# Products of zeros in TensorE's waits, 256-wide chunks in both halves, and a new written order for an attention and two-MoE kernel

## The chip, the core and the metric

The kernel runs on one core of one Trainium2 chip. Its time is device microseconds, from three runs of the kernel before, and one further execution was profiled. A core has TensorE (PE; its weight loads are shown apart as PEld), VectorE (DVE), ScalarE (ACT), GpSimd (POOL) and SyncE (SP), which here issues every DMA. A matrix product writes to PSUM, the accumulators beside it.

## What is computed

Three parts follow each other, all in float32. The inputs q, k, v are 2 batches x 8 heads x 576 positions x 64.

```python
q_d = q.reshape(B, H, Sd, factor, D).mean(axis=3)      # factor = 4; k_d, v_d likewise
out_up = np.repeat(sm_attn(q_d, k_d, v_d), factor, axis=2)
mask = np.abs(pos[:, None] - pos[None, :]) < factor     # a band of 7 positions
out_local = softmax(where(mask, scale * q @ k.T, -1e9)) @ v
x = (out_up + out_local), as 1152 tokens x 512
...
h = x @ w_in                                            # 512 x 2048
x = (h * sigmoid(h)) @ w_out                            # 2048 x 512
...
for e in range(4):                                      # second mixture, w1 512 x 1024, w2 1024 x 512
    out += p[:, e:e+1] * (relu(x @ w1[e]) @ w2[e])
```

## The kernel before

**Products in three passes.** An operand of a large product is split into a high part (fp32r) and the rest: `x` is `xh` and `xl`, a weight is `wh` and `wl`. One product is then three on TensorE: high by high, high by low, low by high (`mm3`, line 603, and line 690 in `quarter`).

**Attention** is cut into 16 jobs, numbered 0 to 15: two batches, two stretches of queries (c = 0 with 256 queries, c = 1 with 320), four pairs of heads. Each job is a round through all engines, whose steps have one letter each, with the job's number behind it:

- S: scores of the band on TensorE and the mask added there (lines 403, 410). x: row maximum and subtraction on DVE (418, 419). e: exp on ACT (424). u: sum on DVE (427).
- q, k, p: q and k summed by fours, q on DVE for the first four jobs, the rest on POOL (365, 342). v: the same for v on POOL. D: scores of the pooled q and k on TensorE (444, 448). n: their maximum on DVE (463, 464). d: their exp on ACT (465).
- r: reciprocals and normalising on DVE (471 to 478). g: the same for the pooled ones on ACT (480). T: transposes on TensorE (490, 492). a: copies of these out of PSUM on ACT (493 to 500).
- V: the values, on TensorE (518, 522). o: a copy on ACT (525). f: the two attentions added on DVE (527). h and l: the sum split into `xh` on ACT and `xl` on DVE (534, 535). tD, tT and the like are the pooled rest of a batch.

**Weights** of the first mixture come as 8 units of 4 pieces, each piece 128 x 512 words of 64 bits, whose two halves hold one float32 weight in a wider form. A piece n (n = 4 x unit + place) is loaded into a stage buffer (`in_s`n) of which there are three, and unpacked in `split_raw`: A on ACT (236), the low word by Z on ACT (242) or, for n in `LOW_ON_DVE`, by B on DVE (239), C on DVE (244), which joins both in a `dec` tile, w on ACT (250) for the high part, L on POOL (251) for the low part.

**The first mixture** runs in two halves of the 2048 columns, each in four chunks of tokens. M and G are products of the first matrix, H of the second: G`c`_`ft`_`k` is chunk c (0 to 3 in half 0, 4 to 7 in half 1), block ft of 128 columns, quarter k of the depth. th, gf, gh and gl are the steps behind a G block (tanh, the product, the split), ya, yf, yh and yl those behind an H block. In half 0 the chunks are 256, 320, 256 and 320 tokens wide, in half 1 256, 256, 256 and 384. M0 to M3 are the blocks of chunk 0 that need one head pair each. Chunks 0 and 1 are done in `quarter` in two parts, so that they can begin while attention still runs.

**The order of the work** around the change is written out by hand. `WRITTEN` holds one list of step names for each of SP, TensorE, ACT, DVE and POOL; `written(names)` chains each step to the one before it, and every engine runs its steps strictly in that order. The lists reach to chunk 5. What is after them (the rest of half 1 and the four experts of the second mixture, lines 603, 843 to 892) is ordered by priorities.

PSUM is shared out as three `mm` tiles, two `s` tiles (scores), `t1` and `t2` (transposes) and `o` (values), each of 128 x 512 float32. A step that writes a tile waits until the tile's last user is done.

Of the kernel before, what the change touches and what calls it, by code (L numbers as in the profile page):

```python
# [62 lines left out]
def attention_moe_kernel(ctx, tc, kqa, kqb, qtl, va, vb, w64, w1d, w2d, dpr, out):  # L63
# [596 lines left out]
    def quarter(ci, p, o, n):  # L660
        c = slice(o, o + n)
        g = [4 * ci + i for i in range(4)]
        two = n == 256
# [15 lines left out]
        for sums in groups:  # L679
            first = {}  # L680
            for i in range(4):
                wh, wl = parts(2 + p, i)
                for d, ps in sums:
                    if not two or len(sums) == 4:
                        next_step(0.125)
                    s = slice(d * 128, d * 128 + 128)
                    h, l = gh[g[i]][:, 0:n], gl[g[i]][:, 0:n]
                    for x, (a, y) in enumerate(((wh, h), (wh, l), (wl, h))):
                        z = two and d % 2
                        m = PE.matmul(out=ps[:, 0:n], lhsT=a[:, s], rhs=y, start=(not z and i == 0 and x == 0),  # L690
                                      stop=(i == 3 and x == 2), skip_group_check=True)
                        if i == 0 and x == 0:
                            first[d] = m
                            if z:
                                after(m, first[d - 1])
                        mark(f"H{ci}_{d}_{4 * p + i}", m)
                if i:
                    attn_tick()
            for d, ps in sums:
                ya = acc[:, d * NT + o:d * NT + o + n]  # L700
                if p == 0:
                    i = ACT.activation(out=ya, in_=ps[:, 0:n], func=ACTF.Copy, scale=0.5)
                else:
                    i = DVE.scalar_tensor_tensor(out=ya, in0=ps[:, 0:n], scalar=0.5, in1=ya, op0=ALU.mult, op1=ALU.add)
                mark(f"ya{ci}_{d}_{p}", i)
# [496 lines left out]
```

## Time and profile before

| what | us |
|---|---|
| median of three runs | 646.92 |
| lowest and highest of them | 645.60 and 648.19 |
| the profiled execution, device time | 649.48 |
| its span, first to last instruction | 647.7 |
| TensorE busy | 629.0 (97%) |
| DVE, ACT, POOL busy | 415.4, 325.3, 249.1 |

The profile is one execution. The page slices the span into 40 equal parts of 16.2 us and gives each a digit, the busy share in tenths. The chain of waits is followed back from the last instruction, at each step to what released it. A timeline row has its start and length in us, the engine, the line, the operation and its tiles, how many such instructions it merges, and in brackets how long the engine was idle before it and what ended that. TensorE's ends are modelled, so the rate of dense products is read from the chain, as the time of many over their number.

### The profile page before, as it was taken

What the parts mean: (1) busy time and instruction counts of PE and PEld (TensorE: products, weight loads), DVE (VectorE), ACT (ScalarE), POOL (GpSimd) and SP (SyncE); (2) the same over time, 40 slices, a digit from 0 to 9 for tenths busy, and PEclk for the clock granted to TensorE, in tenths of its full rate; (3) what the DMA queues carried; (4) which work ended last, traced back from release to release, by engine and by line L of the source; (5) the groups of instructions that cost most, each with busy time, mean ns of one, the idle gap of its engine ahead of it and who ended that gap; (6) DMA issues with size and microseconds to landing.
All of it is one profiled execution on the core that took longest, in us unless ns stands there. A gap on an engine that the chain in (4) does not pass through costs nothing.

```text
span 647.7 us, 13723 instructions
## 1 busy us (share of the span) xinstructions
PE 629.0 (97%) x5492; PEld 617.6 (95%) x5492; DVE 415.4 (64%) x859; ACT 325.3 (50%) x746; POOL 249.1 (38%) x353
## 2 busy tenths in 40 slices
PE   4989999999999999999999999999999999999995
PEld 3779999999999999999999999999999999999995
DVE  5878676547445737756668954769855579755534
ACT  2788776578725525443346533355533366433321
POOL 7567532034400004443646412654433564333210
PEclk9789999999999999999999999999999999999998
DMA  8955551235600400420013300024200020001001
GB/s 276 285 164 187 175 173 56 78 100 163 194 2 1 132 1 1 162 67 2 1 34 108 113 9 1 1 67 131 66 1 2 1 66 1 1 33 35 2 32 50
DMA packets 16928, 48.17 MB, mean 74 GB/s; under 512 B 2976, under 2 KB 4256, under 8 KB 16864
## 3 DMA queue, kind: packets, MB, share of 16 engines
q1 hardware_dynamic: 16864, 47.29, 23.4%
q8 instruction: 43, 0.70, 0.5%
q14 instruction: 21, 0.17, 0.1%
HBM read 44.93 MB, written 2.36 MB: 73 GB/s over the span
## 4 chain that ended last, share of the span: by engine, by line
PE 94%; DVE 3%; ACT 2%; DMA 1%; issue 0%; POOL 0%; ACTq 0%
PE mm L603 57%; PE p L864 27%; PE mm L690 4%; PE s L403 2%; PE o L522 1%; PE t L490 1%; PE o L518 1%; DVE acc L892 1%; DMA kq<-in_kqa_dram 1%; PE mm L993 1%; PE s L410 1%; PE s L448 0%; PE t L492 0%; ACT dec L236 0%; PE mm L403 0%
## 5 line engine op out<-in xcount | busy, mean ns | idle before, releaser
L603 PE MATMUL mm<-xh,wbuf 128*128 128x256 f32 (+2 forms) x1248 | 259.6, 292 | 0.0
L603 PEld LDWEIGHTS mm<-xh,wbuf 128*128 128x128 f32 x1248 | 203.7, 188 | 0.1
L603 PE MATMUL mm<-xl,wbuf 128*128 128x256 f32 (+2 forms) x624 | 182.0, 292 | 0.0
L849 POOL TENSOR_TENSOR r<-r 128x128 f32<-128x128 f32 x160 | 95.0, 606 | 177.4 <-ACT r L843 133.1
L852 DVE TENSOR_TENSOR h<-r,h 128x384 fp32r<-128x384 f32 (+1 forms) x128 | 91.6, 718 | 65.7 <-ACT h L851 65.4
L851 ACT ACTIVATE h<-r 128x384 fp32r<-128x384 f32 (+1 forms) x128 | 73.3, 578 | 93.5 <-POOL r L849 54.5
L603 PEld LDWEIGHTS mm<-xl,wbuf 128*128 128x128 f32 x624 | 117.1, 188 | 0.0
L864 PE MATMUL p<-wext,h 128*128 128x256 f32 x672 | 89.2, 276 | 0.0
L864 PE MATMUL p<-wbuf,h 128*128 128x256 f32 x672 | 82.7, 276 | 0.0
L864 PEld LDWEIGHTS p<-wext,h 128*128 128x128 f32 x672 | 82.2, 188 | 0.0
L864 PEld LDWEIGHTS p<-wbuf,h 128*128 128x128 f32 x672 | 79.4, 188 | 0.0
L603 PE MATMUL mm<-gh,wbuf 128*128 128x256 f32 (+2 forms) x384 | 77.1, 292 | 0.0
L603 PEld LDWEIGHTS mm<-gh,wbuf 128*128 128x128 f32 x384 | 62.0, 188 | 0.0
L843 ACT ACTIVATE r<-mm 128x512 f32<-128x512 f32 x48 | 28.6, 596 | 65.4 <-PE mm L603 64.7
L849 DVE TENSOR_TENSOR r<-r 128x128 f32<-128x128 f32 x96 | 39.3, 410 | 34.0 <-ACT r L843 29.4
L603 PE MATMUL mm<-gl,wbuf 128*128 128x256 f32 (+2 forms) x192 | 55.8, 291 | 0.0
L631 DVE TENSOR_TENSOR gl<-gf,gh 128x256 fp32r<-128x256 f32 (+2 forms) x64 | 34.2, 540 | 18.1 <-ACT gh L630 17.7
L625 DVE SCALAR_TENSOR_TENSOR gf<-th,mm 128x256 f32<-128x256 f32 (+2 forms) x64 | 28.7, 451 | 23.6 <-ACT th L624 21.6
L251 POOL TENSOR_TENSOR wbuf<-dec,wbuf 128x512 fp32r<-128x512 f32 x24 | 31.0, 1301 | 26.4 <-ACT wbuf L250 20.4
L892 DVE SCALAR_TENSOR_TENSOR acc<-p,pr,acc 128x256 f32<-128x256 f32 (+1 forms) x63 | 36.1, 605 | 3.6 <-PE p L864 3.0
L794 POOL TENSOR_TENSOR wext<-kst,wext 128x512 fp32r<-128x512 f32 x8 | 10.4, 1300 | 69.5 <-ACT wext L792 46.9
L630 ACT ACTIVATE gh<-gf 128x256 fp32r<-128x256 f32 (+2 forms) x64 | 28.0, 442 | 16.5 <-DVE gf L625 15.7
(173 smaller groups left out, 1035.2 us busy)
## 6 DMA issues: line engine op xcount, KB each, us to landing
stg<-in_w_dram SPq DMA_DIRECT2D x29, 512.0 KB
kst<-in_w2d_dram SPq DMA_DIRECT2D x16, 512.0 KB
kst<-in_w1d_dram SPq DMA_DIRECT2D x12, 512.0 KB
kq<-in_kqb_dram SPq DMA_DIRECT2D x8, 323.0 KB
kq<-in_kqa_dram SPq DMA_DIRECT2D x6, 419.0 KB
stg<-in_w1d_dram SPq DMA_DIRECT2D x4, 512.0 KB
acc<-in_w_dram SPq DMA_DIRECT2D x3, 512.0 KB
vw<-in_vb_dram SPq DMA_DIRECT2D x8, 180.0 KB
```

What stands on the lines that cost most here:

```text
L251: mark(f"L{4 * u + j}", POOL.tensor_tensor(out=l, in0=d, in1=h.bitcast(F32), op=ALU.subtract))
L603: ins = [PE.matmul(out=ps, lhsT=l, rhs=r, start=(first and i == 0), stop=(last and i == n - 1)) for i, (l, r) in enumerate(pairs)]
L625: mark(f"gf{c}_{ft}", DVE.scalar_tensor_tensor(out=gf[:, 0:n], in0=th[:, 0:n], scalar=1.0, in1=ps[:, 0:n], op0=ALU.add, op1=ALU.mult))
L630: latest[ACT] = mark(f"gh{c}_{ft}", ACT.activation(out=gh[g][:, 0:n], in_=gf[:, 0:n], func=ACTF.Copy))
L631: latest[DVE] = mark(f"gl{c}_{ft}", DVE.tensor_tensor(out=gl[g][:, 0:n], in0=gf[:, 0:n], in1=gh[g][:, 0:n].bitcast(F32), op=ALU.subtract))
L690: m = PE.matmul(out=ps[:, 0:n], lhsT=a[:, s], rhs=y, start=(not z and i == 0 and x == 0), stop=(i == 3 and x == 2), skip_group_check=True)
L843: ACT.activation(out=r[:, 0:4].rearrange("p s t -> p (s t)"), in_=ps[:, 0:512], func=ACTF.Relu)
L849: latest[eng] = eng.tensor_tensor(out=r[:, o], in0=r[:, a], in1=r[:, b], op=op)
L851: ACT.activation(out=h, in_=r[:, part], func=ACTF.Copy)
L852: latest[DVE] = DVE.tensor_tensor(out=l, in0=r[:, part], in1=h.bitcast(F32), op=ALU.subtract)
L864: ins = [PE.matmul(out=ps, lhsT=x, rhs=y, start=(opens and k == 0 and i == 0), stop=(k == 3 and i == n - 1), skip_group_check=True) for i, ...
L892: DVE.scalar_tensor_tensor(out=o, in0=ps, scalar=p, in1=o, op0=ALU.mult, op1=ALU.add)
```

## The change

Four things change.

1. **Chunks.** Both halves now use 256, 256, 256 and 384 tokens. `quarter` loses its form for 320 tokens, with its groups of three and one PSUM tiles; four 256-wide sums now share two tiles in both of its chunks. The tiles `gh`, `gl`, th and gf are opened 256 wide, and 384 wide from the last chunk of half 0 on.
2. **Products of zeros.** `fill(name, t)` issues `FILL[name]` matrix products of a 128 x 128 by a 128 x 256 bf16 tile of zeros ahead of a step, into the PSUM tile that the step is about to write. There are 39. The zeros lie in an unused part of `acc`, cleared on DVE by the first step there, `cw`.
3. **Unpacking.** Pieces 16 to 31 (units 4 to 7) take their low word by B on DVE instead of Z on ACT. For these units the `dec` tile is gone: A writes to the upper words of the stage buffer, and C, w and L work on it there.
4. **Written order.** All five lists are new, and reach one chunk further, to the new chunk 5 and the loads and splits of the first expert weights (`in_w9_1`, `in_k0_0` to `in_k0_2`, `hw`, `lw`).

```diff
-XN = (256, 320, 256, 320)
-
-CHUNKS = (tuple(zip(XOFF, XN)), ((0, 256), (256, 256), (512, 256), (768, 384)))
+CHUNKS = ((0, 256), (256, 256), (512, 256), (768, 384))
...
-LOW_ON_DVE = (0, 1, 2, 3)
+FILL = {"S2": 4, "S4": 4, "V0": 6, "T1": 5, "V2": 2, "S6": 1, "T5": 3, "V5": 5, "T6": 9}
+LOW_ON_DVE = (0, 1, 2, 3) + tuple(range(16, 32))
...
-            d = d_p.tile([128, 512], F32, tag="dec", name="dec")
+            d = d_p.tile([128, 512], F32, tag="dec", name="dec") if u < 4 else v[:, :, 1].bitcast(F32)
...
+    zeros = acc[:, 4470:4598].bitcast(BF16)
+
+    def fill(name, t):
+        for _ in range(FILL.get(name, 0)):
+            mark(name, PE.matmul(out=t, lhsT=zeros[:, 0:128], rhs=zeros, start=True, stop=True, skip_group_check=True))
+
     def constants():
+        mark("cw", DVE.memset(zeros, 0.0))
...
+        fill(f"S{j.i}", j.ps[:, 0:256])
...
+        fill(f"T{j.i}", t1[:, 0:2].rearrange("p a b -> p (a b)"))
...
+        fill(f"V{j.i}", o[:, 0:256])
...
-        two = n == 256
...
-        if two:
-            b = [mm_tile() for _ in range(2)]
-            groups = [[(d, half(b[d // 2], d % 2)) for d in range(4)]]
-        else:
-            groups = [[(d, mm_tile()) for d in ds] for ds in ((0, 1, 2), (3,))]
+        b = [mm_tile() for _ in range(2)]
+        sums = [half(b[d // 2], d % 2) for d in range(4)]
...
-    open_g(320)
+    open_g(256)
...
+            if hf == 0 and lastc:
+                m1ctx.close()
+                open_g(384)
...
-            if (hf, ci) == (1, 1):
+            if (hf, ci) == (1, 2):
                 for names in WRITTEN:
                     written(names)
...
-        if hf == 0:
-            m1ctx.close()
-            open_g(384)
```

The beginnings of the five lists, SP, TensorE, ACT, DVE and POOL in turn:

```diff
-        """in_kq0 in_kq1 in_s0 in_kq2 in_vg0 in_kq3 in_vg1 in_kq4 in_kq5 in_vw0 in_s1 in_qt in_vg3 in_vw1 in_s3 in_vg2 in_vw2
-        in_s2 in_kq6 in_s8 in_s10 in_vw3 in_kq7 in_s9 in_vg8 in_vw4 in_kq12 in_vw5 in_kq8 in_s11 in_vg9 in_kq9 in_s4
+        """in_kq0 in_kq1 in_s0 in_s1 in_kq2 in_kq3 in_kq4 in_vg0 in_vg1 in_vw0 in_s2 in_kq5 in_vw1 in_vw2 in_s3 in_qt in_s9
+        in_vg2 in_vg3 in_s8 in_vw4 in_kq6 in_vw5 in_s10 in_vw3 in_kq7 in_vg8 in_kq8 in_kq12 in_s11 in_kq9 in_vw6 in_vg9
...
-        """S0 S1 D0 D1 S2 S3 T0 D2 S4 V0 S5 T1 D3 D5 D4 V1 M0 T2 M1 V2 T3 tD S6 T4 V3 D6 S7 M2 tT M3 V4 T5 D7 S8 T6 V5 D8
-        H0_0_0 H0_2_0 H0_3_0 S9 H0_1_0 H0_0_1 H0_2_1 V6 T7 G1_0_0 H0_1_1 D9 H0_3_1 G1_0_1 G1_0_2 V7 S10 H0_0_2 H0_2_2 T8
+        """S0 S1 D0 S2 D1 S3 T0 S4 D2 V0 T1 S5 D4 V1 D3 M0 T2 D5 M1 V2 T3 tD S6 T4 M2 V3 S7 D6 tT T5 V4 D7 M3 S8 V5 S9 T6 D8
+        H0_0_0 H0_1_0 H0_2_0 H0_3_0 T7 V6 H0_0_1 G1_0_0 G1_0_1 H0_2_1 H0_1_1 H0_0_2 H0_1_2 G1_0_2 H0_3_1 V7 S10 D9 T8
...
-        """e0 A0 e1 d0 d1 e2 g0 a0 tab w0 o0 d2 g1 e3 A1 h0 e4 e5 a1 w1 d3 o1 d4 g2 h1 a2 d5 g3 A2 g4 A3 o2 a3 Z8 w3 h2 g5
+        """tab A0 e0 A1 e1 w0 d0 g0 d1 g1 e2 a0 w1 d2 e3 o0 e4 h0 A2 a1 A3 o1 e5 h1 d3 g2 d4 w2 a2 d5 Z9 g3 g4 o2 A8 a3 h2 g5
...
-        """x0 q0 q1 x1 n0 cz B0 C0 n1 q2 u0 r0 x2 u1 q3 r1 x3 n2 x4 f0 u2 B1 x5 C1 l0 n3 r2 n4 u3 f1 n5 u4 l1 r3 r4 u5 B3 r5
+        """cw cz q0 q1 x0 B0 x1 C0 B1 n0 C1 q2 u0 r0 n1 x2 u1 r1 x3 n2 x4 B2 f0 u2 q3 r2 l0 x5 n4 B3 f1 n3 C2 u3 l1 u4 n5 r3
...
-        """cb ci cq cm k0 k1 v0 k2 v1 k3 p4 p5 tp L0 L1 v2 v3 L3 p6 L2 p7 L8 v8 p8 L9 p9 L10 v9 L11 p10 p11 L4 v10 v11 L6 L5
+        """cq cb cm ci k0 k1 L0 k2 v0 p4 v1 L1 k3 p5 tp v2 L2 v3 L3 p6 p7 L9 v8 p8 L8 v9 L10 p9 v10 L11 p10 p11 L5 L4 p12 L6
```

## Rows read from the trace of the kernel before

**Rows 1.** The page's slices of the span: TensorE busy, its granted clock, transfers.

```profile
PE   4989999999999999999999999999999999999995
...
PEclk9789999999999999999999999999999999999998
...
GB/s 276 285 164 187 175 173 56 78 100 163 194 2 1 132 1 1 162 67 2 1 34 108 113 9 1 1 67 131 66 1 2 1 66 1 1 33 35 2 32 50
```

**Rows 2.** Busy us by stage: PE, PEld, DVE, ACT, POOL, granted clock, DMA share, GB/s.

```profile
4.00:16.00 12.00, 7.88 (x80) 5.58 (x80) 8.44 (x21) 3.50 (x9) 9.26 (x16) 1.00 1.00 318
16.00:24.00 8.00, 7.33 (x82) 5.73 (x82) 5.76 (x17) 4.55 (x14) 2.78 (x8) 0.57 0.96 264
24.00:37.00 13.00, 10.65 (x155) 9.09 (x152) 11.57 (x39) 11.86 (x35) 10.17 (x13) 1.00 0.60 203
...
48.00:123.00 75.00, 75.00 (x830) 70.70 (x831) 53.66 (x140) 55.28 (x153) 31.91 (x47) 1.00 0.45 140
...
123.00:180.00 57.00, 56.96 (x458) 56.53 (x457) 29.48 (x55) 42.99 (x94) 20.63 (x16) 1.00 0.45 140
```

**Rows 3.** The chain of waits, TensorE's dense stretches: start, us, what.

```profile
108.57 5.29 PE mm L690 x36
...
302.90 2.72 PE mm L603 x24
...
350.74 4.16 PE mm L603 x24
```

**Rows 4.** Timeline of ACT, the first exp.

```profile
6.97 1.28 ACT L424 ACT_TABLE_LOAD   x1 [6.97 <-DVE s L419]
8.27 0.39 ACT L424 ACTIVATE s<-s 128x280 f32<-128x280 f32 x1
```

**Rows 5.** Timeline of DVE, unpacking: lines 239 (B) and 244 (C).

```profile
10.04 1.24 DVE L239 TENSOR_SCALAR stg<-stg 128x512 int32<-128x512 int32 x1
...
11.39 1.56 DVE L244 SCALAR_TENSOR_TENSOR dec<-dec,stg 128x512 int32<-128x512 int32 x1
...
22.04 0.42 DVE L239 TENSOR_SCALAR stg<-stg 128x512 int32<-128x512 int32 x1
...
23.84 0.68 DVE L244 SCALAR_TENSOR_TENSOR dec<-dec,stg 128x512 int32<-128x512 int32 x1
```

**Rows 6.** Timeline of TensorE: S0, T0, V0, M0, S6, the first H.

```profile
4.37 1.20 PE L403 MATMUL s<-kq 64*64 64x70 f32 x16 [4.37 <-DMA kq<-in_kqa_dram]
...
15.02 0.63 PE L490 MATMUL t<-ident,sm 128*70 128x128 f32 x4 [1.88 <-DVE sm L478]
...
19.49 0.70 PE L518 MATMUL o<-atd,vd 72*64 72x64 f32 x8
...
26.15 0.39 PE L993 MATMUL mm<-xh,wbuf 128*128 128x256 f32 x1
...
31.90 0.83 PE L403 MATMUL s<-kq 64*64 64x70 f32 x20
...
48.25 0.38 PE L690 MATMUL mm<-gh,wbuf 128*128 128x256 f32 x1
```

**Rows 7.** The chain of waits, M2 and M3.

```profile
38.79 2.15 PE mm L993 x12
41.16 1.38 PE mm L993 x12
```

**Rows 8.** Timeline of POOL: a v step, an L step, the last eight L.

```profile
9.96 1.04 POOL L342 TENSOR_TENSOR vg_f<-vg_f 72x512 f32<-72x512 f32 x1 [1.52 <-DMA vg_f<-in_va_dram]
...
33.53 1.28 POOL L251 TENSOR_TENSOR wbuf<-dec,wbuf 128x512 fp32r<-128x512 f32 x1 [2.29 <-ACT wbuf L250]
...
158.59 2.56 POOL L251 TENSOR_TENSOR wbuf<-dec,wbuf 128x512 fp32r<-128x512 f32 x2 [3.10 <-ACT wbuf L250]
...
172.44 2.54 POOL L251 TENSOR_TENSOR wbuf<-dec,wbuf 128x512 fp32r<-128x512 f32 x2 [1.58 <-ACT wbuf L250]
```

**Rows 9.** Groups by line: Z.

```profile
L242 ACT ACTIVATE stg<-stg 128x512 int32<-128x512 uint16 x26 | 17.4, 674 | 2.2 <-DMA stg<-in_w_dram 2.2
```

More of the change, by code (lines that the diff above doesn't have):

```diff
@@ L257, in split_raw @@
             c = slice(j * 1024, (j + 1) * 1024)
-            behind(ACT, ACT.activation(out=h[:, c], in_=t, func=ACTF.Copy))
-            behind(DVE, DVE.tensor_tensor(out=l[:, c], in0=t, in1=h[:, c].bitcast(F32), op=ALU.subtract))
+            mark(f"hw{u}_{j}", ACT.activation(out=h[:, c], in_=t, func=ACTF.Copy))
+            mark(f"lw{u}_{j}", DVE.tensor_tensor(out=l[:, c], in0=t, in1=h[:, c].bitcast(F32), op=ALU.subtract))
     actx = ExitStack()
@@ L672, in quarter @@
         flush()
-        if two:
-            b = [mm_tile() for _ in range(2)]
-            groups = [[(d, half(b[d // 2], d % 2)) for d in range(4)]]
-        else:
-            groups = [[(d, mm_tile()) for d in ds] for ds in ((0, 1, 2), (3,))]
-        step[0] -= 0.5
[L679 to L705, printed above, removed]
@@ new lines, in quarter @@
+        b = [mm_tile() for _ in range(2)]
+        sums = [half(b[d // 2], d % 2) for d in range(4)]
+        step[0] -= 0.5
+        first = {}
+        for i in range(4):
+            wh, wl = parts(2 + p, i)
+            for d, ps in enumerate(sums):
+                next_step(0.125)
+                s = slice(d * 128, d * 128 + 128)
+                h, l = gh[g[i]], gl[g[i]]
+                for x, (a, y) in enumerate(((wh, h), (wh, l), (wl, h))):
+                    m = PE.matmul(out=ps, lhsT=a[:, s], rhs=y, start=(d % 2 == 0 and i == 0 and x == 0),
+                                  stop=(i == 3 and x == 2), skip_group_check=True)
+                    if i == 0 and x == 0:
+                        first[d] = m
+                        if d % 2:
+                            after(m, first[d - 1])
+                    mark(f"H{ci}_{d}_{4 * p + i}", m)
+            if i:
+                attn_tick()
@@ L707, in g2_evac @@
+        for d, ps in enumerate(sums):
+            ya = acc[:, d * NT + o:d * NT + o + n]
+            if p == 0:
+                i = ACT.activation(out=ya, in_=ps, func=ACTF.Copy, scale=0.5)
+            else:
+                i = DVE.scalar_tensor_tensor(out=ya, in0=ps, scalar=0.5, in1=ya, op0=ALU.mult, op1=ALU.add)
+            mark(f"ya{ci}_{d}_{p}", i)
     def g2_evac(hf, db, c, ps, n):
@@ L775, in split_u @@
             with at_prio(tick_of(e, 0, k) - LEAD_USPLIT):
-                ACT.activation(out=h[:, c], in_=t[:, c], func=ACTF.Copy)
+                mark(f"uh{e}_{k}_{c.start}", ACT.activation(out=h[:, c], in_=t[:, c], func=ACTF.Copy))
                 eng = POOL if k in U_LO_POOL else DVE
-                eng.tensor_tensor(out=l[:, c], in0=t[:, c], in1=h[:, c].bitcast(F32), op=ALU.subtract)
+                mark(f"ul{e}_{k}_{c.start}", eng.tensor_tensor(out=l[:, c], in0=t[:, c], in1=h[:, c].bitcast(F32),
+                                                               op=ALU.subtract))
         held[i] -= 1
@@ new lines, in attention_moe_kernel @@
+        C6 gl1_2 x12 gf1_3 n11 f9 C7 u11 gl1_3 r11 l9 gf0_4 n12 C13 u12 C12 gl0_4 f10 gf0_5 r12 l10 x13 gf0_6 gl0_5 gf0_7
+        nt1 gl0_7 C14 rt1 C15 gf1_4 gl0_6 x14 gf1_5 ya0_2_1 f11 ya0_3_1 gl1_4 l11 n13 gl1_5 gf1_6 n14 ya0_0_1 B16 gl1_6
+        gf1_7 u13 gl1_7 ya0_1_1 r13 ya1_0_1 ya1_1_1 f12 B17 x15 gf2_0 l12 u14 n15 gf2_1 r14 gl2_0 gl2_1 u15 f13 gf2_2 C16
+        r15 gf2_3 B18 gl2_2 l13 gf2_4 ya1_2_1 ya1_3_1 gl2_3 f14 gf2_5 C17 gl2_5 l14 C18 gl2_4 gf2_6 gf2_7 f15 gl2_6 gl2_7
+        l15 B20 B19 C19 C20 B21 gf3_0 C21 gf3_1 gl3_0 gl3_1 gf3_2 gf3_3 gl3_3 gf3_4 gl3_4 B22 C22 gf3_5 gl3_2 gf3_6 B23
@@ L989, in start_mm @@
             hold.extend(mm_tile() for _ in range(2))
+            fill("M0", hold[0][:, 0:256])
         for i in range(4):
@@ L1053, in attention_moe_kernel @@
                         load_piece()
-        for ci, (o, n) in enumerate(CHUNKS[hf]):
+        for ci, (o, n) in enumerate(CHUNKS):
             if hf == 0 and ci < 2:
                 continue
-            lastc = ci == len(CHUNKS[hf]) - 1
+            lastc = ci == len(CHUNKS) - 1
+            if hf == 0 and lastc:
+                m1ctx.close()
+                open_g(384)
             main_at[1] = 4 * hf + ci
```

100 lines of the change are left out of this document (52 added, 48 removed).

## The prediction

> **What bounds the kernel now.** I read the page's slices first, then the stages, then the chain of waits and the timelines of the first 50 us. The reader is to see that TensorE is full in every slice but the first, the third and the last, that its granted clock is below full only near the start (0.7 and 0.8 in the second and third slice), and that the transfers run at 276 GB/s there [rows 1]. The stages say where time can still be won [rows 2]: from 48 us on TensorE is busy to within 0.04 us, so the end moves only with the work that it is given there; before 48 us it idles, or runs slowly, for part of the time. In 24:37 ACT (11.86 of 13.00) and DVE (11.57) are nearly full, but in 16:24 they are not (4.55 and 5.76 of 8.00), and in 4:16 ACT is busy for 3.50 of 12.00. The ramp up to the first H product at 48.25 [rows 6] is therefore bound first by a chain of steps through all engines, and then by ACT and DVE.
>
> The profiled execution took 649.48 us, 647.7 of them span. The median of the runs shown is 646.92. I work the sum in microseconds off the profiled execution and take it off the median unscaled.
>
> **Chunk widths.** The 384 products of half 0 that are 320 wide become 192 of 256 and 192 of 384; half 1 is unchanged, and so is the number of products. The chain of waits, where it is dense, gives 5.29/36 = 147 ns for 320, 2.72/24 = 113 ns for 256 and 4.16/24 = 173 ns for 384 [rows 3]. Before: 384 x 147 = 56.4 us. After: 192 x (113 + 173) = 55.0. This stands on the dense path: **-1.4 us**.
>
> **Table load.** ACT loads its table only when the first exp is due: 6.97 to 8.25, and the exp starts at 8.27; what released the load was DVE's subtraction for that same exp [rows 4]. With `tab` first in ACT's order, after the DVE memset `cz`, the load falls into the empty microseconds before the first scores at 4.37 [rows 6]: -1.3 on the first chain. It is the first term of the ramp, not to be added to it. The one load of the trace is followed at once by the exp, so nothing but its 1.28 us is on the path. The Trainium skill, ScalarE: Activation LUTs, "What ACT_TABLE_LOAD costs", adds a drain of 1.38 us to a load of 1.28; the row agrees with the load and shows no drain on the path. By that page the gain would be 2.7 and the forecast 1.4 lower, 640.1; I take the row.
>
> **The order of the ramp**, walked step by step through the new orders with the old durations.
> - First scores: S0 and x0 stay, e0 comes at about 7.4 behind A0 instead of 8.27, D0 at 7.85. DVE now has B0, x1, C0 and B1 ahead of n0; at 0.42 for a B and 0.68 for a C [rows 5] n0 starts near 9.2 and the first normalised scores are ready at 11.8. Before, T0 waited for them until 15.02 [rows 6], as B0 and C0 took 1.24 and 1.56 there while POOL added v [rows 5, 8].
> - T0 stands behind S2, D1 and S3. s1, now fourth on SP instead of eleventh, delays kq2 by its 128 x 512 words of 8 bytes, 0.52 MB, at 276 GB/s [rows 1]: 1.9 us. So S2 starts at 9.6, S3 ends near 13, T0 starts at 13.1: 1.9 us ahead of 15.02 [rows 6].
> - V0: S4 and its four zero products follow T0 instead of D2; v0 waits for vg0, which lands some 4.6 us later (s1, kq3 and kq4, 1.28 MB, pass it), and ends at 15.1. V0 starts at 16, 3.5 ahead of 19.49 [rows 6].
> - M0: l0 has fewer steps ahead of it on DVE (C1 and the maximum after S5 have moved) and ends by 19.5. M0 then waits for D3, whose k3 is queued behind L0 and L1 on POOL at 1.28 each [rows 8]: 21.1 against 26.15 [rows 6].
> - From there the shift can't grow, for ACT and DVE are full. A3 waits some 0.3 us on ACT for s3; v2 waits on POOL for vg2, with L2 and v3 queued behind it. On SP kq8 is moved ahead of kq12, which waits there for kq6's buffer and held up all loads behind it, so S8 no longer waits for that. M3 comes at 36.5 (before 41.16 [rows 7], less what runs ahead of it), the first H product at 42.7 against 48.25.
> So the walk gives 5.6 us at that product, and S9 (at most 0.83, what 20 products took at full clock [rows 6]) has by then been done too: 6.4. Against it I set 1.7 us, since two DVE steps were that much longer beside POOL [rows 5] and four such steps now stand there, and 0.7 us for late landings and steps that just miss. **-4.0 us**. The bounds are -1.3 (the table load alone, then ACT and DVE full as before) and -6.4.
>
> **Zero products.** 39 products of 256 columns, written to a tile that the next step overwrites. I price one by the 113 ns row, 4.4 us in all, or at the lower clock by M2's twelve in 2.15 [rows 7], 0.18 each, 7.0 us. They wait for the PSUM tile and not for the data, so they lie in front of steps whose data come later: S2 for kq2, V0 for a0 and v0, T6 for D8's p8 behind it. What covers them is the lateness of DVE, ACT and POOL; where that is gone they cost their full price and S4, T1 or V5 is late next. What they may give is the clock: in 16:24 it was 0.57 of full [rows 2], that is 6.9 of the 8 us at 1.2 GHz and the rest at 2.4, after 12 us in which TensorE had been busy for 7.88; and M2 took 2.15 against M3's 1.38 [rows 7]. My walk has full clock from about 12.5, so both the price and the gain are in it. Bounds of this item: 7.0 lost; gained 3.4 (half of the 6.9) and 0.8 (M2).
>
> **Edits at nothing.** B16 to B31 put 16 x 0.42 = 6.7 us on DVE and take 16 x 0.67 [rows 9] off ACT. All of it is in 123:180, where DVE has 29.48 of 57.00 and TensorE is full [rows 2]. A writes in place at a stride; Z does that already [rows 9], so no price. But a stage buffer is now held until L on POOL (1.28) instead of until C. The last eight L took from 158.59 to 174.98 [rows 8], 2.05 each; w and L, 1.9 us more for one of three buffers, make it 2.7, 21.6 for the eight of units 6 and 7. Between the G3 products that free their place and chunk 4's H products, their users, stand H3's 96 products at 173 ns and G4's at 113, 27.5 us. Bounds 0 and 2 us late; I take 0, for the rest that this leaves. The wider g pool is opened one chunk earlier; it makes the first gh of chunk 3 wait for the last H of chunk 2 in place of the same wait one chunk later, and the new order has G3 products between them. The longer order and the named expert loads concern the stretch after 180, where TensorE stays full [rows 1]. The zeros' memset runs on DVE before the first scores.
>
> **Sum.** -1.4 - 4.0 = -5.4: 649.48 becomes 644.1, the median 646.92 becomes **641.5**.
>
> **The rivals.**
> - ACT and DVE are the bound (20%). What the first 20 us win is lost by 37 us, since the same work must pass ACT at 11.86 of 13.00. For: the full engines in 24:37 [rows 2]. Against: ACT's idle time before 24, into which A1, A2 and w1 now move. It leaves the table load and the widths: 646.92 - 2.7 = 644.2.
> - The zeros don't hold the clock (10%). In 16:24 TensorE was busy for 7.33 of 8.00 and the granted clock was 0.57 [rows 2], so busy time alone did not keep it up. Then the low stretches stay, 4.2 us by the bounds above, of which I let 1.7 hide in waits: 641.5 + 2.5 = 644.0. The Trainium skill, TensorE: Matmul & The Clock Gate, "Part 4: PE-mode transpose", says that transposes don't engage the full clock, which would leave T's stretches low whatever stands beside them; no row here separates T from its neighbours.
> - Filler runs out, **slower** (9%). Chunk 1 loses 64 columns: 192 products x (147 - 113) = 6.5 us that stood between attention steps now come after them. ACT needs 55.28 us of the 75.00 in 48:123 [rows 2]; in 68.5 that is 81%, which speaks against it. But if the latency of a job's round, not the volume, sets the pace, TensorE idles for all 6.5 and the ramp gives only the load: 646.92 + 6.5 - 2.7 = 650.7. It decides if TensorE waits for ACT or DVE between 48 and 115 us, by more than about 4 us.
> - `tab` makes no early load (3%): if the copy were served by one table and the exp by another, a second load would stay before e0, and 1.3 of the ramp with it: 642.8. The trace has one load for exp, copy and tanh, which speaks against it.
>
> **How the numbers follow.** The forecast has 58%, 641.5, with its own range 638.5 to 643.6. The rivals above take 42%. The range goes down to 638.0 (the full walk with few losses, 646.92 - 7.8 - 1) and up to 646.0, past the first two rivals with the stage buffers' 2 us; what is left out is mostly the slower case. 0.5% is 3.2 us, about what a measurement of this kernel tells from no change. Faster by more (below 643.7): the forecast, the small rival and a little of the others, 0.63. Within: the first two rivals, 0.28. Slower: 0.09.
>
> **What would show it.** Right: the table load before 4 us; the first M product near 21 to 23, the first H product at 42 to 45; granted clock higher in 16:24; no TensorE gap after; the end at 641 to 643. Wrong: zero products with steps queued behind them whose data were ready; ACT or DVE above 95% from 15 to 40; TensorE gaps between 48 and 115, or before the first H of half 1.

## The result and the profile after

The changed kernel takes **655.09 us** (median), the kernel before on the same chip 647.34: a ratio of 1.0119, 95% interval 1.0082 to 1.0155. It is slower by some 7.7 us where 5.4 less were forecast. Medians are of all executions; ratios, intervals and spreads leave out the few much longer ones of a kernel, here one of the changed kernel's six (668.93). The profiled execution took 654.13 us, span 652.3, against 649.48 and 647.7.

The page of the changed kernel first: slices of TensorE and of its granted clock [rows 1], and the head of the chain that ended last.

```profile
PE   6888999999999799999999999999999999999995
...
PEclk9999999999999999999999999999999999999998
...
PE 83%; DMA 9%; issue 3%; DVE 2%; POOL 1%; ACT 1%; SPq 0%; POOLq 0%; ACTq 0%
```

The page shows no granted clock below full before the last slice. (The rows say that the rate was about half up to some 13 us all the same: four products of zeros took 1.03 us at 9.05 and 0.60 at 14.08.) TensorE's first slice is fuller (6 for 4), the second and the fourth are not (8 for 9), and a new 7 stands in slice 14, where before all was 9. The chain now goes through transfers for 9% (before 1%). The stages of [rows 2], and one more, 210:230, in the changed kernel (same columns: sum, PE, PEld, DVE, ACT, POOL, granted clock, DMA share, GB/s):

```profile
4.00:16.00 12.00, 10.65 (x115) 7.66 (x115) 9.93 (x27) 5.26 (x15) 8.57 (x15) 1.00 1.02 325
16.00:24.00 8.00, 7.85 (x112) 6.46 (x111) 7.41 (x23) 6.09 (x21) 7.35 (x13) 1.00 0.99 296
24.00:37.00 13.00, 9.88 (x144) 8.32 (x143) 8.66 (x26) 9.47 (x28) 7.46 (x11) 1.00 0.92 241
48.00:123.00 75.00, 73.24 (x858) 69.85 (x858) 55.19 (x148) 55.65 (x158) 30.83 (x46) 1.00 0.39 125
123.00:180.00 57.00, 56.63 (x414) 56.12 (x413) 31.64 (x59) 32.16 (x68) 19.53 (x14) 1.00 0.41 121
210.00:230.00 20.00, 15.96 (x134) 15.16 (x132) 12.61 (x25) 9.01 (x20) 1.30 (x1) 1.00 0.33 107
```

In 24:37 it is the transfers that are full (0.92, before 0.60), while ACT fell from 11.86 to 9.47 and DVE from 11.57 to 8.66. And TensorE stands still for 4.04 of 20 us in 210:230, where the kernel before has 20.00:

```profile
210.00:230.00 20.00, 20.00 (x179) 20.00 (x178) 13.54 (x30) 10.11 (x23) 1.29 (x1) 1.00 0.37 107
```

An account of all of TensorE's time makes the sum: every interval from one product's start to the next counts for the step of the first one, so waits are in it. Worked out from the two traces (us):

| part | before | after | forecast of the difference | measured |
|---|---|---|---|---|
| attention steps, M, zeros | 66.72 | 67.76 | -4.0 | +1.0 |
| G and H of chunks 0 to 3 | 99.22 | 98.35 | -1.4 | -0.9 |
| chunk 4 to the last product | 470.20 | 474.91 | 0 | +4.7 |
| before the first, after the last start | 11.57 | 11.33 | 0 | -0.2 |
| span | 647.71 | 652.35 | -5.4 | +4.6 |

The profiles differ by 4.6 us and the ratio says 7.7, since two single executions stand here. That of the kernel before took 649.48, 2.3 above the mean of its six; that of the changed kernel took 654.13, 0.7 below the mean of its five without the longest. The former had a mean granted clock of 0.990; of 105 executions of this kernel beside the experiments only five were as low, and their mean is 0.995. So the first row shows too little of what the ramp lost: e8 below, one edit away from the kernel before and profiled close to its median, has 63.85 us there, 3.9 less than the changed kernel.

**The stretch after 210.** Four lines of TensorE's timeline in the changed kernel, with the idle time before each and what ended it:

```profile
217.95 0.28 PE L612 MATMUL mm<-xh,wext 128*128 128x256 f32 x1
219.53 0.39 PE L612 MATMUL mm<-xh,wext 128*128 128x256 f32 x1 [1.31 <-DVE gf L634]
...
221.91 0.39 PE L612 MATMUL mm<-xh,u 128*128 128x256 f32 x1 [0.69 <-DVE gf L634]
...
225.54 0.38 PE L612 MATMUL mm<-xh,u 128*128 128x256 f32 x1 [1.98 <-DVE gf L634]
```

The products of chunk 6 wait for an accumulator, which `gf` frees once `th` has been taken. `th` is ACT's L633. ACT at that time:

```profile
210.21 1.05 ACT L257 ACTIVATE wbuf<-stg 128x1024 fp32r<-128x1024 f32 x1
214.30 0.42 ACT L719 ACTIVATE xh<-gf 128x256 fp32r<-128x256 f32 x1 [3.04 <-DVE gf L717]
216.18 2.01 ACT L257 ACTIVATE wbuf<-stg 128x1024 fp32r<-128x1024 f32 x2 [1.46 <-DMA stg<-in_w1d_dram]
218.10 0.40 ACT L719 ACTIVATE xh<-gf 128x256 fp32r<-128x256 f32 x1
218.40 0.36 ACT L633 ACTIVATE th<-mm 128x256 f32<-128x256 f32 x1
```

L257 is `hw`, the copy of the next mixture's weights, which the written order now names. `hw9_1` waits 1.46 us for its load, `hw9_0` follows, and only then `yh5_3` and the first `th` of chunk 6. The load can't come earlier: SP issues it when `lw8_1` on DVE has freed a stage buffer. On DVE `lw9_1` and `lw9_0` then stand ahead of the next `gf`, 2.35 us:

```profile
212.54 0.33 SPq L202 DMA_DIRECT2D stg<-in_w1d_dram  x1
```

```profile
222.46 2.35 DVE L258 TENSOR_TENSOR wbuf<-stg,wbuf 128x1024 fp32r<-128x1024 f32 x2
```

**The ramp.** TensorE's timeline in the changed kernel: T0, V0's zeros, M0, V2, S6, S7, M3, V5's and T6's zeros, the first H.

```profile
13.31 0.72 PE L498 MATMUL t<-ident,sm 128*70 128x128 f32 x4
...
16.03 0.83 PE L284 MATMUL o<-acc 128*128 128x256 bf16 x6
...
21.63 0.39 PE L1006 MATMUL mm<-xh,wbuf 128*128 128x256 f32 x1
...
27.02 0.46 PE L527 MATMUL o<-atd,vd 72*64 72x64 f32 x8 [0.93 <-POOL vd L348]
...
30.54 0.83 PE L410 MATMUL s<-kq 64*64 64x70 f32 x20 [1.22 <-DMA kq<-in_kqb_dram]
...
35.85 0.83 PE L410 MATMUL s<-kq 64*64 64x70 f32 x20 [0.80 <-DMA kq<-in_kqb_dram]
...
40.12 0.38 PE L1006 MATMUL mm<-xh,wbuf 128*128 128x256 f32 x1
...
43.18 0.71 PE L284 MATMUL o<-acc 128*128 128x256 bf16 x5 [0.46 <-DVE xl L544]
...
45.69 1.15 PE L284 MATMUL t<-acc 128*128 128x256 bf16 x9
...
47.59 0.38 PE L693 MATMUL mm<-gh,wbuf 128*128 128x256 f32 x1
```

Up to M0 the walk holds: 13.1, 16 and 21.1 were forecast, 13.31, 16.03 and 21.63 came, M0 4.5 us ahead of [rows 6]. By M3 (40.12; 36.5 forecast, 40.91 before) nearly all of it is lost, and what stands in between are waits for transfers: V2 behind `vg2`, S6 behind kq6, S7 behind kq7. M3 in the kernel before:

```profile
40.91 0.37 PE L993 MATMUL mm<-xh,wbuf 128*128 128x256 f32 x1
```

SP had issued kq6 and kq7 long before their use:

```profile
20.23 0.35 SPq L127 DMA_DIRECT2D kq<-in_kqb_dram  x1
...
25.14 0.35 SPq L127 DMA_DIRECT2D kq<-in_kqb_dram  x1
```

From 20.23 to S6 at 30.54, and from 25.14 to S7 at 35.85, a load of 323 KB took over 10 us, behind the pieces of weights s9 and s8, which the order of before issues after kq6. And with the attention 4.5 us ahead at M0, both loads were issued no earlier than in the kernel before, where kq7 went out at 23.50 and kq6 at 20.18:

```profile
20.18 0.35 SPq L128 DMA_DIRECT2D kq<-in_kqb_dram  x1
```

ACT met such pieces too (table load, `tab`, A0, A3):

```profile
0.73 1.28 ACT L302 ACT_TABLE_LOAD   x1 [0.73 <-PEq L1204]
2.03 0.31 ACT L302 ACTIVATE qdl<-zero 128x128 f32<-128x128 f32 x1
7.27 0.67 ACT L235 ACTIVATE dec<-stg 128x512 f32<-128x512 f32 x1 [4.93 <-DMA stg<-in_w_dram]
...
21.27 0.67 ACT L235 ACTIVATE dec<-acc 128x512 f32<-128x512 f32 x1 [1.10 <-DMA acc<-in_w_dram]
```

### The profile page after: what moved, and what is told of

It reads as the page before. It is cut to its first block, busy times and chain, and to the rows that moved or that the text cites. A ratio compares the mean times of both kernels' runs of the same rounds, so it can differ in the third digit from the quotient of the medians.

```text
span 652.3 us, 13815 instructions
## 1 busy us (share of the span) xinstructions
PE 630.0 (97%) x5531; PEld 617.7 (95%) x5531; DVE 425.5 (65%) x876; ACT 317.8 (49%) x730; POOL 252.8 (39%) x353
## 4 chain that ended last, share of the span: by engine, by line
PE 83%; DMA 9%; issue 3%; DVE 2%; POOL 1%; ACT 1%; SPq 0%; POOLq 0%; ACTq 0%
PE mm L612 52%; PE p L868 27%; PE mm L693 2%; DMA vw<-in_va_dram 2%; DMA kq<-in_kqb_dram 2%; DMA kq<-in_kqa_dram 2%; DMA vg_f<-in_va_dram 1%; DMA stg<-in_w_dram 1%; PE s L410 1%; DMA vg<-in_va_dram 1%; POOL wext L250 1%; DVE acc L896 1%; DMA kst<-in_w2d_dram 1%; PE o L531 0%; DMA vw<-in_vb_dram 0%
## 5 line engine op out<-in xcount | busy, mean ns | idle before, releaser
L612 PE MATMUL mm<-xh,wbuf 128*128 128x256 f32 (+1 forms) x1248 | 259.5, 292 | 0.4 <-ACT acc L714 0.4
L612 PE MATMUL mm<-xl,wbuf 128*128 128x256 f32 (+1 forms) x624 | 181.9, 292 | 0.0
L612 PE MATMUL mm<-gh,wbuf 128*128 128x256 f32 (+1 forms) x384 | 79.0, 296 | 0.1
L612 PE MATMUL mm<-gl,wbuf 128*128 128x256 f32 (+1 forms) x192 | 56.7, 296 | 0.0
L634 DVE SCALAR_TENSOR_TENSOR gf<-th,mm 128x256 f32<-128x256 f32 (+1 forms) x64 | 28.7, 452 | 25.6 <-ACT th L633 25.1
L640 DVE TENSOR_TENSOR gl<-gf,gh 128x256 fp32r<-128x256 f32 (+1 forms) x64 | 37.6, 593 | 10.9 <-ACT gh L639 10.5
L633 ACT ACTIVATE th<-mm 128x256 f32<-128x256 f32 (+1 forms) x64 | 26.0, 409 | 26.3 <-PE mm L612 25.7
L639 ACT ACTIVATE gh<-gf 128x256 fp32r<-128x256 f32 (+1 forms) x64 | 27.8, 442 | 18.9 <-DVE gf L634 18.8
L612 PEld LDWEIGHTS mm<-gl,wbuf 128*128 128x128 f32 x192 | 36.0, 188 | 0.0
```

The source lines that it names most:

```text
L612: ins = [PE.matmul(out=ps, lhsT=l, rhs=r, start=(first and i == 0), stop=(last and i == n - 1)) for i, (l, r) in enumerate(pairs)]
L633: mark(f"th{c}_{ft}", ACT.activation(out=th[:, 0:n], in_=ps[:, 0:n], func=ACTF.Tanh, scale=0.5))
L634: mark(f"gf{c}_{ft}", DVE.scalar_tensor_tensor(out=gf[:, 0:n], in0=th[:, 0:n], scalar=1.0, in1=ps[:, 0:n], op0=ALU.add, op1=ALU.mult))
L639: latest[ACT] = mark(f"gh{c}_{ft}", ACT.activation(out=gh[g][:, 0:n], in_=gf[:, 0:n], func=ACTF.Copy))
L640: latest[DVE] = mark(f"gl{c}_{ft}", DVE.tensor_tensor(out=gl[g][:, 0:n], in0=gf[:, 0:n], in1=gh[g][:, 0:n].bitcast(F32), op=ALU.subtract))
```

## The experiments

Thirteen kernels ran beside the kernel before; a ratio is always to that kernel on the same chip, with its 95% interval. The expectations call a piece of weights of the first mixture, with its steps A, Z, B, C, w and L, an expert half, and the copies `hw`, `lw` expert steps.

**1 to 4: the tail of the order, and the zeros.**

```diff
 # e1: the changed kernel, out of the written order (ACT, DVE, SP) and background work again as before
-hw8_0 hw8_1 hw9_0 hw9_1   lw8_0 lw8_1 lw9_0 lw9_1 sh   in_w9_1 in_k0_0 in_k0_1 in_k0_2
 # e2: the changed kernel;  e3: e1
-FILL = {"S2": 4, "S4": 4, "V0": 6, "T1": 5, "V2": 2, "S6": 1, "T5": 3, "V5": 5, "T6": 9}
+FILL = {}
 # e4: the kernel before, with fill() and this FILL, cw first on DVE
```

> Theory 1: TensorE's gaps at 218 to 230 us of the changed kernel (1.5, 0.9 and 2.2 us, with smaller ones about 5 in all) come from the tail of the written order: ACT holds yh5_3 and the first th of chunk 6 behind hw9_1, and hw9_1 waits for a load that can be issued only when lw8_1 has freed its stage buffer. With the expert splits of units 8 and 9, the shares and their loads taken out of the written lists (placed as in the kernel before), the gaps go and the time falls by 5 us, to about 650. Rival: chunk 6 is late for another reason, the splits move elsewhere and the gap with them; the time stays at 654 to 655.

Measured: 652.3, ratio 1.0053 (1.0027 to 1.0079). Of the tail's three waits two were left, shorter:

```profile
217.80 0.39 PE L612 MATMUL mm<-xh,wext 128*128 128x256 f32 x1 [0.71 <-DVE gf L634]
...
223.99 0.39 PE L612 MATMUL mm<-xh,u 128*128 128x256 f32 x1 [0.28 <-DVE gf L634]
```

> The changed kernel without its 39 products of zeros, all else the same. Theory 2: they stand on TensorE's path for most of their price, 39 x 0.11 = 4.4 us, and the clock needs them little; the time falls by 2 to 4 us, to 651 to 653. Rival: they keep the granted clock full between 16 and 41 us; without them the low stretches of the kernel before return, and the time rises by 2 to 4 us, to 657 to 659, or stays if price and clock cancel.

Measured: 654.64, ratio 1.0091 (1.0055 to 1.0127); the waits after 210 stayed.

> Both edits. If theories 1 and 2 hold and add up: 655 - 5 - 3 = 647, the time of the kernel before. If only theory 1 holds: 650. If the zeros keep the clock: 652 or more.

Measured: 649.19, ratio 1.0038 (1.0007 to 1.0068).

> The kernel before with the same 39 products of zeros at the same steps, and its own written order, chunks and unpacking. Theory 2: some of their 4.4 us stands on the path and some of the low clock in 16:24 and 37:40 goes; 647 to 651. Rival (clock first): 643 to 645, as up to 4.2 us of low clock go and the zeros lie in waits.

Measured: 648.5, ratio 1.001 (0.9983 to 1.0038). The clock of 0.57 in 16:24 [rows 2] is gone in this kernel, and nothing is won by it:

```profile
16.00:24.00 8.00, 7.44 (x110) 5.55 (x112) 5.68 (x17) 5.17 (x16) 5.82 (x13) 1.00 1.01 253
```

What follows: the tail of the order costs several microseconds, and the zeros hold the clock in the executions profiled so far without earning their time.

**5, 6, 8, 9: the whole length of the order, the order of the loads, the table load alone.**

```diff
 # e5: the changed kernel with every list cut after chunk 4, where those of before end (no G5, H5, th5, gh5, ..., hw, lw, sh, in_w9_1, in_k0)
-            if (hf, ci) == (1, 2):
+            if (hf, ci) == (1, 1):
 # e6: e5 with another order of loads (and kq11 ahead of s6, A8 behind w3);  e9: e6 with FILL = {}
-in_s9 in_vg2 in_vg3 in_s8 in_vw4 in_kq6 in_vw5 in_s10 in_vw3 in_kq7
+in_vg2 in_kq6 in_vg3 in_s9 in_vw3 in_vw4 in_vw5 in_kq7 in_s8 in_s10
 # e8: the kernel before; cz first on DVE and on ACT
-e0 A0 e1 d0 d1 e2 g0 a0 tab w0
+tab e0 A0 e1 d0 d1 e2 g0 a0 w0
```

> The kernel after with the written order cut where the one of before ends (chunk 4), and the expert loads, their copies and subtractions background work again. Theory 1 (the longer order makes the late waits, all of them): none of the TensorE gaps between 211 and 240 us is left, also not the 0.87 and 0.45 us that stayed when only the expert steps were freed; the gain over that run is 1.5 to 1.7 us, 650.6 by medians; instructions of the two kernels in step from 240 us on. Rival (those two waits come with the widths or the stage buffers): they stay and the median stays at 652.3 within 1 us.

Measured: 651.07, ratio 1.0045 (1.0015 to 1.0074). The stretch after 210 is whole again:

```profile
210.00:230.00 20.00, 20.00 (x178) 20.00 (x178) 13.74 (x30) 10.80 (x24) 1.29 (x1) 1.00 0.37 107
```

From chunk 4 on the account gives 469.69 us, before 470.20, after 474.91. The two short waits of e1 have gone as well, so theory 1 holds for all of them: the longer order costs 5.2 us in the profiles (474.91 - 469.69), and by ratios 1.0119 - 1.0045, or 4.8, with an uncertainty of some 3. Up to chunk 4 the changed kernel, e1 and e5 do the same work in the same order, and M3 comes at 40.12, 39.03 and 41.51: a difference of 2 us in the ramp between two single profiles says nothing.

> As the run with the order cut at chunk 4, and in the ramp vg2, kq6, vw3 and kq7 are issued ahead of the expert halves s9, s8, s10, kq11 ahead of s6, and ACT's A8 moved behind w3. Theory 2 (the ramp of after waits for transfers that stand in the wrong order): the waits of TensorE for v2 (1.09 us), S6 (1.39), S7 (0.91) and S11 (1.22) go, M3 starts at 36.5 to 38 us instead of 40.1, and the median falls by 2 to 4 us against the run beside it, to some 647. Rival (ACT and DVE are the bound in the ramp): M3 moves by less than 1 us, and the median stays within 1 us of that run.

Measured: 649.96, ratio 1.0019 (0.9992 to 1.0047), 1.1 below e5 by medians (1.7 by ratios) where 2 to 4 were expected. S6 came at 29.54 and no longer waited for its load. But ACT did: 1.92 us before Z9 and 1.30 before A8, and M3 at 38.99 was not early.

> The kernel before with one edit: cz first on DVE and tab first on ACT. By my first term the load of the table (1.28 us) leaves the first chain: e0 ends and D0 starts 1.3 us earlier, and as far as that shift lasts the median falls from 647.7 to 646.4. Rival (what comes next is bound by transfers or by ACT and DVE): D0 is 1.3 us earlier but S6 and M3 start where they did, and the median stays at 647.7 within 0.5.

Measured: 646.93, ratio 0.9984 (0.9966 to 1.0002). D0, T0, M3 and the first H of this kernel:

```profile
7.48 0.74 PE L444 MATMUL s<-kd,qp 64*64 64x144 f32 x4
...
13.15 1.06 PE L490 MATMUL t<-ident,sm 128*70 128x128 f32 x4
...
36.11 0.37 PE L947 MATMUL mm<-xh,wbuf 128*128 128x256 f32 x1
...
44.61 0.38 PE L690 MATMUL mm<-gh,wbuf 128*128 128x256 f32 x1
```

D0 is 1.28 us earlier (8.76 before) and T0 1.87 [rows 6]. In this execution M3 is ahead by 4.8 and the first H by 3.6, but its granted clock was 1.00 up to 64 us, where the profiled execution of before had 0.57 in 16:24, so this is not the table load alone; by medians 1.1 are left, and the interval takes in no change. So this one edit stands below e5, the whole change without its tail.

> As the run with the order cut and the loads reordered, without the 39 zero products. Theory 3 (the zeros cost more TensorE time than the clock gives back, as 652.3 against 649.2 with only the expert steps freed): some 2 to 3 us below the run beside it, 644 to 645, below both kernels. Rival (they keep the clock up and pay for themselves, as 648.5 against 647.7 in the kernel before): within 1 us of it, with a granted clock below full in parts of 16 to 40 us.

Measured: 647.75, ratio 0.9994 (0.9977 to 1.0011). The zeros' removal brought 2.2 us by medians (1.6 by ratios), near theory 3; but the kernel is level with the one before and not below it.

**10, 11, 13, 14: the pieces of weights behind the attention steps.**

```diff
 # e11: e5;  e10: e9;  e13: e6, each with, on ACT and DVE
-tab A0 e0 A1 e1 ... a1 A3 o1 e5 h1 d3 ... d5 Z9 g3 g4 o2 A8 a3 h2 g5 w3 Z8 e6 dt0 A9 gt0
+tab e0 A0 e1 A1 ... a1 o1 e5 h1 A3 d3 ... d5 g3 g4 o2 a3 h2 g5 Z9 w3 A8 Z8 e6 dt0 A9 gt0
-x0 B0 x1 C0 B1 n0 C1
+x0 x1 n0 B0 C0 B1 C1
 # (the first line is that of e5: in e9 and e6 A8 stands behind w3 already; and B3 just before C2); e14: e10 with, on ACT (and C9 just before C8 on DVE)
-g5 Z9 w3 A8 Z8 e6 dt0 A9 gt0
+g5 w3 e6 dt0 gt0 Z9 A8 Z8 A9
```

> As the run with the order cut, the loads reordered and no zeros, and ACT and DVE take the steps of the expert halves behind the attention steps that stood after them: A0 after e0, A1 after e1, A3 after h1, Z9 after g5, x1 and n0 before B0, B3 before C2. Theory 4 (in the new order attention steps queue on ACT behind steps that wait for an expert half to land: A0 4.76 us, A3 1.83, Z9 2.54 in the run without these moves): these waits go, e0 starts at 7.0 instead of 7.7, M3 at 36 to 38 instead of 40.9, and the median falls by 1.5 to 3 us against that run's 647.75, to 645 to 646. Rival (DVE or POOL is the bound in the ramp, and the waits only cover it): ACT waits for DVE at the same places, M3 within 1 us of 40.9, median within 0.7 of 647.75.

Measured: 648.67, ratio 1.0019 (0.9997 to 1.0041): a miss. A0's and A3's waits went and e0 came early, but the wait had only moved. ACT and TensorE of this kernel:

```profile
34.20 0.65 ACT L235 ACTIVATE dec<-acc 128x512 f32<-128x512 f32 x1 [1.98 <-DMA acc<-in_w_dram]
```

```profile
36.76 1.43 PE L410 MATMUL s<-kq 64*64 64x70 f32 x20 [2.67 <-ACT dec L235]
```

A8 waits for s8, with e6 and dt0 queued behind it, and S7 waits for these.

> As the run with the order cut at chunk 4 (zeros and the change's own order of loads kept), with the same moves on ACT and DVE as the run beside it. Theory 4: the waits of e0 and of o1 and e5 behind A0 and A3 go, 651.07 falls by 1 to 2 us; the waits of TensorE for v2, S6, S7 and S11, which belong to the order of the loads, stay (some 4 us together). Rival: no change, within 0.7 us.

Measured: 650.11, ratio 1.0037 (1.0017 to 1.0057), 1.0 below e5 by medians and 0.5 by ratios: not to be told from no change, which was the rival. ACT now waited for no landing longer than 0.25 us before 50 us, and TensorE's waits for loads stayed (S6 1.98, S11 1.33 us).

> As the first run of this call with the 39 zeros kept. Theory 3 (their price is above what the clock gives back where TensorE's waits are short): 1.5 to 2.5 us above the first run, as 649.96 stood to 647.75. Rival (the zeros only stretch executions whose loads land late; without steps queued behind such loads they cost nothing): within 1 us of the first run, and the spread of its executions shrinks from the 10.7 us of the run with the loads reordered to about 4.

Measured: 653.38, ratio 1.0074 (1.0046 to 1.0103), 4.7 above e10 by medians and 3.6 by ratios, uncertain by more than 2. The rival fell; whether the zeros cost more here than the 1.5 to 2.5 us of theory 3 can't be told.

> As the run with late halves, reordered loads and no zeros, with Z9, A8, Z8 and A9 behind gt0 on ACT and C9 just before C8 on DVE. Theory 4 (attention steps queue on ACT behind landings of expert halves; the moves before only shifted the place from A3 and Z9 to A8): A8's wait no longer stands before e6 and dt0, S7's wait of 2.78 us on TensorE goes, and the median falls from 648.67 by 2 to 3 us to some 646. Rival (the transfers are the bound up to the first H product, in whatever order ACT meets them): S7 starts earlier, but o3 and a4 or the first H products then wait for A8, A9 and w8, the first H product stays at 47 to 50 us, and the median stays within 1 us of 648.67.

Measured: 649.8, ratio 1.0023 (1.0002 to 1.0044). The rival holds (its median is 1.1 above e10's where it said at most 1). S7 did start at 32.24, 4.5 us earlier, and then the tail's transposes waited for what stands behind A8:

```profile
34.62 0.66 ACT L235 ACTIVATE dec<-acc 128x512 f32<-128x512 f32 x1 [1.70 <-DMA acc<-in_w_dram]
```

```profile
37.44 0.41 PE L513 MATMUL t<-ident,ed 128*72 128x128 f32 x2 [3.55 <-ACT atd L508]
```

The first H came at 48.62. s8 was issued at 23.11 and its step began at 34.62. Wherever ACT meets these pieces, something of the ramp waits for them.

**12: the widths in the order of before.**

```diff
 # e12: the changed kernel's code with the lists of e8; B16 to B31 for Z16 to Z31, FILL = {};
 # H1 in pairs of a bank, H1_3_6, H1_2_7 and H1_3_7 behind G2_1_3, H2_3_5 to 7 behind G3_0_2, ya steps to match
```

> The order of before with the table load first, and half 0 in chunks of 256, 256, 256, 384 (with what belongs to it: B for units 4 to 7, in-place steps, the g pool one chunk earlier), without zeros; the H products of chunk 1 in pairs of a bank, and the last H2 products before the second G3 block. My term of the widths says -1.4 us, the sums over the two profiles say -0.9 to -1.1: 646.93 falls to 645.5 to 646.0, below both kernels. Rival (chunk 1's 6.5 us less of filler, or the held stage buffers, show up as TensorE waits between 48 and 215 us): 647 or more, with such waits in the trace.

Measured: 660.07, ratio 1.0198 (1.017 to 1.0226). A miss that says little of the widths: my own re-sorting of chunks 1 to 3 left waits at their seams, from a profiled execution that was longer than the median:

```profile
72.29 0.38 PE L692 MATMUL mm<-gl,wbuf 128*128 128x256 f32 x1 [0.63 <-DVE gl L639]
...
78.85 0.66 PE L454 MATMUL s<-kd,qbd 128*128 128x144 f32 x2 [1.74 <-ACT s L430]
```

TensorE idles 9.2 us between 48 and 210 in it. By its letter the rival holds, for such waits are what it said; the run can't tell it from my re-sorting. The widths were therefore measured only inside the other kernels. By the account chunks 0 to 3 take 97.98 to 98.64 us in those with the zeros (after, e1, e5, e6, e11, e13) and 98.95 to 99.39 in those without (e2, e3, e9, e10, e14), against 99.22 before.

## Why the prediction was wrong

**The step that failed.** "The longer order and the named expert loads concern the stretch after 180, where TensorE stays full [rows 1]", at a price of nothing. That TensorE was full there rested on background work that gave way: `hw` and `lw` ran when ACT and DVE had nothing else (the four copies at 208.90, 210.16, 213.37 and 215.36, the next `th` at 216.31). Written into the queues at fixed places they can wait with others behind them. I walked the new order only to 48 us and never asked of `hw9_1` what is queued behind it while it waits. The price was 5.2 us; e5 shows it by taking it away, and e1 got 3.3 of it back (the account says 471.57 from chunk 4 on) by freeing the expert steps alone. Of the 10.0 us between the forecast and the two profiles 4.7 are this, and 5.0 the ramp.

**The ramp, the second error.** The walk was right as far as M0 and wrong from "M3 comes at 36.5". I let the shift of 5 us stand because ACT and DVE were full in 24:37, and set 0.7 us for late landings. [rows 2] had the transfers' share at 1.00 and 0.96 in 4:24, and I read no bound in it. With the attention earlier they stayed full through 24:37 (0.92): V2, S6 and S7 lost 0.93, 1.22 and 0.80 us on TensorE and A3 1.10 on ACT, so that S6 came only 1.36 us earlier than before [rows 6], where M0 had been 4.5 ahead. The sum was +1.0 instead of -4.0. e6, e10 and e14 changed the order in which the loads and pieces were met, and the wait moved each time: shown for these orders. That fewer bytes would free the ramp is argued, not tried; and bytes alone are not the bound, for e8 moves the same ones in the order of before and has its first H at 44.61, ahead of every kernel with the new order (45.02 in e2 to 50.22 in e10). What in the new order costs the rest is open.

**The table load** was right as a mechanism: D0 moved by 1.28, and e0 there (e8) starts 0.1 us behind the subtraction that it needs, so nothing more was there to win. The drain of 1.38 us that the Trainium skill, ScalarE: Activation LUTs, "What ACT_TABLE_LOAD costs", adds to the load was not on this path.

**The widths** were right in the changed kernel: -0.9 against -1.4. Some 0.5 is a new wait of chunk 3's first products for an accumulator. In the kernels without zeros this row gains 0.3 at most: there the first H block takes 1.3 to 1.5 us instead of 0.5, a wait that is covered where T6's zeros stand before it.

**The zeros** at nothing: inside the bounds, but not nothing. Five pairs of kernels with and without them differ by 0.0028 (after, e2), 0.0015 (e1, e3), 0.0025 (e6, e9), 0.0055 (e13, e10) and 0.001 (e4, before) in ratio, always against the zeros: 0.6 to 3.6 us, 1.6 in the middle, each uncertain by 2 to 3. The sentence "they wait for the PSUM tile and not for the data" failed where the tile comes last. V5's five zeros start when the accumulator is free, its data long there, and T6's nine take 0.99 us (45.69 to the transposes at 46.68) in front of ready steps. Yet here they cost next to nothing, since the second H product needs `gl0_0` from DVE and would have waited. It comes 4.63 us after V5's zeros begin at 43.18, and in e2, without zeros, 4.45 after V5 begins; e3 and e9 have the same 4.45 and 4.44. The changed kernel, then e2:

```profile
47.81 0.31 PE L693 MATMUL mm<-gl,wbuf 128*128 128x256 f32 x1
```

```profile
41.69 0.50 PE L527 MATMUL o<-atd,vd 72*64 72x80 f32 x8 [0.55 <-DVE xl L544]
...
46.14 0.39 PE L693 MATMUL mm<-gl,wbuf 128*128 128x256 f32 x1 [0.74 <-DVE gl L640]
```

In the order of e10 it takes 3.40 us, and with the zeros, in e13, 4.54: there the same fourteen cost 1.1. Where the other 25 cost theirs is not shown. Nor was there much clock to win, as the unusual clock of the profiled execution had made me think: over all executions behind the ratios the mean granted clock of these pairs is between 0.0004 lower and 0.0022 higher with the zeros, by my estimate (0.0022 x 648) 1.4 us at the most.

**The rivals.** "The zeros don't hold the clock" fell: 16 to 48 us ran at 1.00 in after, e1, e4, e5 and e6, and the clock was low somewhere there in before, e2, e3, e9, e10, e12 and e14, one execution each. They don't always do so (e11 0.87 and e13 0.91 in 24:37, with waits of 1.98 and 2.66 us in that stretch), and e8 had 1.00 without them. T's transposes stood in these full stretches. So the rule of the Trainium skill, TensorE: Matmul & The Clock Gate, "Part 4: PE-mode transpose", that transposes don't engage the full clock, did not show in the granted clock. "ACT and DVE are the bound" had the right place and the wrong resource: both are less busy in 24:37 than before. "Filler runs out" forecast the sign for a wrong reason: TensorE idled 1.76 us of 48:123, under my 4 us, and 1.10 of it was S11 waiting for kq11's transfer. "`tab` makes no early load" fell: the one load starts at 0.73. The chance of 0.09 for slower left out that a part costed at nothing can have a price.

**The other edits at nothing.** B16 to B31, the in-place step and the longer-held stage buffer left no mark that I can see: TensorE has 56.63 of 57.00 in 123:180, and chunk 4's first H comes at 181.34 (before 181.06). No run tries them alone. My reading that all sixteen Z stood in 123:180 was wrong for three of them (106.7 to 110.6 in the kernel before).

**A better version.** None beats the kernel before by more than its measurement can tell. The nearest are e8 (0.9984, up to 1.0002) and e9 (0.9994). What stays open is whether the widths could be had in e8's order, well sorted, and for how much.

## What to carry to other kernels

Work that fills gaps in the background cost nothing here because it gave way; named in a fixed order it needs its own walk, with its load and the buffer that lets the load start. When a ramp is shortened, look first at the share of the transfers and at when each load goes out: here, at 0.9 and more, reordering steps moved the wait about. A filler is paid for where the step behind it is ready and nothing soon after has to wait anyway: the same fourteen cost 0.2 us in one order and 1.1 in another. And before pricing a cure for a slow stretch of one profile, see how often other executions have it.

## What was not expected of the hardware

**Landing times.** With the 16 engines at a share of 0.9 to 1.0, a load of 323 to 512 KB was used 10 to 11.5 us after its issue (kq6, kq7, s8 of e14). The Trainium skill, DMA: Bandwidth & Descriptors, "Queues, rings and completion order", says that each engine takes the descriptors of a ring in order; the trace of the changed kernel agrees, for A8 took s8, issued before kq6, at 28.23, and S6 took kq6 at 30.54.

**Two speeds at full clock.** Three profiled executions ran the dense products of 256 columns at 118 ns instead of 113, with a granted clock of 1.00, in stretches without a wait: e3 from about 225 to 335 us, e13 from about 180 to 335, and e12 from about 180 to its end. The rows are e1's and e3's, 179 and 172 products in the same 20 us, and a late one of e12's:

```profile
290.00:310.00 20.00, 20.00 (x179) 20.00 (x178) 11.10 (x22) 7.29 (x13) 5.74 (x10) 1.00 0.00 1
```

```profile
290.00:310.00 20.00, 20.00 (x172) 20.00 (x171) 9.60 (x18) 5.80 (x11) 5.18 (x9) 1.00 0.00 1
```

```profile
610.00:630.00 20.00, 20.00 (x172) 20.00 (x172) 10.14 (x20) 6.95 (x13) 5.29 (x10) 1.00 0.08 27
```

It is worth some 3 us in e3 and 4 to 5 in e13 by the account, and e12's profiled execution took 675.33 us, 15 more than its median. Its cause is open, and a single profile can't be set against another without looking for it.

**Spread.** Ten executions of e6 took 645.51 to 652.38 us (two more 655.38 and 656.2), twelve of e9 645.5 to 648.95, with the same order of loads. A median of a few runs of such a kernel is worth 1 to 2 us, no less.
